# Attention with a token-mixer gate on one core: PSUM banks in one turn for scores and products, product blocks spread evenly, a tail in half-array products

## The chip, the cores and the metric

The kernel runs on one core of a Trainium2 chip. TensorE (PE) multiplies out of SBUF into eight PSUM banks of 128 x 512 fp32. VectorE (DVE), ScalarE (ACT) and GpSimd (POOL) read and write beside it, and SyncE (SP) issues most transfers. The metric is device time in microseconds (us), the median of the runs shown.

## The reference

`x` is 2048 tokens by 512 channels. With `xn = layernorm(x)` the kernel computes

```
s = softmax(q k^T / 4) v @ wo        # 32 heads of 16 channels, q, k, v = xn @ wqkv
g = silu((gelu(layernorm(xn)^T @ w1 + b1) @ w2 + b2)^T)   # a mixer over the tokens, F = 1792
out = x + s * g
```

All inputs are fp32. A product is made of three fp32r products of upper and lower parts (`three`, or the triple loops in `mixer` and `products`), so that every matrix product costs three passes.

## The kernel before, in words

**Opening (chunks of 512 tokens, `for c in range(NC)`).** Four blocks of 128 tokens are normalized (`Norm`: `stats`, `rsqrt`, `apply`, from L196 on), turned by TensorE (`turned`, L264), split into upper and lower parts, and multiplied with the weights of q and k (L303, eight groups of 12 passes) and of v (`v_product`, L336). q, k and v go to DRAM.

**Steady part (`for s in range(0, total + 1, 2)`).** The heads are taken in 16 pairs, `a` = 0 and 1, which use the upper and the lower half of the PE array's rows at the same time. One turn of the loop is a double step. For step `s` it makes the scores whose row maxima are sought (`max_of`: TensorE L394 into bank pool `ps_mx`, reduced by DVE L398), and, `LEAD` = 22 steps later, the scores again with the maximum folded in (`score`: TensorE L777 into `ps_sc`, exponentials by ACT L782). `values` (L793) multiplies the exponentials with v, four column tiles at once, into `ps_av`. A double step therefore has eight `m` (maxima), eight `s` (scores), two `V` (values), and `n` passes of the other work.

That other work is one long list (`everything`: `mixer`, then `rest`). It is drawn with `take` and consists of **blocks**: 14 of 48 passes (first matrix of the mixer, closed by `gelu`), 16 of 42 (second matrix, closed by `silu`), then 9 passes per output block (`products` with three of four head groups, closed by `part`), and at last the remaining 3 or 12 passes per output block (closed by `finish`). All passes of a block add up in one PSUM bank, `dn`. In the steady part each pass is split into two halves of 64 rows, `D` (`halves`, L944), one for each half of the array, so that every `D` runs beside an `m`, an `s` or another `D`. Outside the steady part it is one pass of 128 rows (`whole`, L903).

The order of a double step is written by hand in the strings of `ORDERS`: two rows of letters, one for each half of the array, read column by column, so one column is a pair of matmuls that run together; the two numbers are the columns before which a `V` stands. `count` says how many passes a double step takes: 6 as a rule, and 4 where a block ends or has just ended (`late`, with the tables `ENDS` and `BEGINS`), because the next block must wait until the single bank `dn` has been read out.

**PSUM.** Four pools: `ps_sc` 3 banks, `ps_mx` 3, `ps_av` 1, `ps_dn` 1.

**Tail (`else` branch, s >= NU = 512).** No maxima are left. Per half of a double step come score pairs, a `V` and up to 12 whole passes, three where an output block needs only its last head group. After the last `V` the last pair of heads is divided, multiplied with its share of `wo`, gated, added and stored (L1087 to the end).

Of the kernel before, what the change touches and what calls it, by code (L numbers as in the profile page):

```python
# [21 lines left out]
def tile_attention_token_mixer(ctx, tc, x, wqkv, wo, w1, b1, w2, b2, out):  # L22
# [131 lines left out]
    with (  # L154
        tc.tile_pool(name="pw", bufs=1) as pw,
        tc.tile_pool(name="px", bufs=5) as px,
        tc.tile_pool(name="pt", bufs=6) as pt,
# [23 lines left out]
        for part in range(3):  # L181
            for kd in range(ND):
                nm = ("raw", "wh", "wl")[(part * ND + kd) % 3]
# [4 lines left out]
        def w_upper(part):  # L188
            for kd in range(ND):
                nc.scalar.copy(wh[part][:, kd, :], raw_w[part, kd])  # L190

        def w_lower(part):
            for kd in range(ND):
                sub(nc.gpsimd, wl[part][:, kd, :], raw_w[part, kd], wh[part][:, kd, :])

        class Norm:  # L196


            def __init__(self, src, dst, then=None):
                self.src, self.dst, self.then = src, dst, then  # L200
# [7 lines left out]
            def rsqrt(self):  # L208
                ve = pst.tile([P, 4], F32, name="ve")
                r = self.r = pst.tile([P, 4], F32, name="r")  # L210
                t = pst.tile([P, 4], F32, name="t")
                nc.vector.tensor_scalar(ve, self.mv[:, :, 1], 1e-5, None, op0=OP.add)
                nc.scalar.sqrt(t, ve)
                nc.vector.reciprocal(r, t)
# [14 lines left out]
            def pieces(self):  # L229
                for b in range(4):  # L230
                    yield lambda b=b: self.stats(b)
                yield self.rsqrt
                for b in range(4):
                    yield lambda b=b: self.apply(b)

        def first(c):
# [4 lines left out]
            return Norm(lambda b: xr[4 * c + b], dst)  # L241
# [11 lines left out]
        def bank():  # L253

            i = turn_of[0] = (turn_of[0] + 1) % 8
            pl, nm = ((ps_sc, "sc"), (ps_mx, "mx"), (ps_dn, "dn"), (ps_av, "av"))[i % 2 if i < 6 else i - 4]
            return pl.tile([P, 512], F32, name=nm)

        for f in first(0).pieces():
            f()  # L260
        w_upper(0)
        xts_ = [[] for _ in range(NC)]

        def turned(c, db):  # L264
# [4 lines left out]
            t = pt.tile([P, 2, 512], F32R, name="xt")  # L269
            nc.scalar.copy(t[:, 0, :], ps)  # L270
            sub(nc.vector, t[:, 1, :], ps, t[:, 0, :])
            xts_[c].append(t)

        for c in range(NC):
            cs = slice(c * 512, (c + 1) * 512)
            for db in range(len(xts_[c]), ND):
                turned(c, db)
            if c == 0:

                nc.gpsimd.tensor_copy(pst.tile([P, 1], F32, name="hold"), xn[3][:, :1])  # L280
                w_upper(1)
                w_lower(0)
                w_lower(1)
# [5 lines left out]
            if c == 0:  # L289
                w_upper(2)  # L290
                w_lower(2)
# [35 lines left out]
            for f in todo[len(order) * per :]:  # L327
                f()
# [11 lines left out]
            pv = [bank()[:, :D] for _ in range(4)]  # L340
            if c + 1 < NC:
                for kd in range(ND):
                    for b in range(4):
                        v_product(b, kd)
                    if 0 < kd < ND - 1:
                        turned(c + 1, kd + 1)
            for b, ps in enumerate(pv):
# [5 lines left out]
                else:  # L353
                    v48 = pt.tile([P, 2, 512], F32R, name="xt").bitcast(F32).rearrange("p a b -> p (a b)")
                    v48 = v48[:, : NP * 48].rearrange("p (a b c) -> p a b c", b=3, c=DH)
                nc.gpsimd.memset(v48[:, :, 1, :], 1.0)
                nc.scalar.copy(v48[:, :, 0:3:2, :], ps.rearrange("p (a b c) -> p a b c", b=2, c=DH))
                nc.sync.dma_start(v_d[4 * c + b], v48.rearrange("p a b c -> p (a b c)"))
# [76 lines left out]
    def mixer():  # L435
        n = 0
        ub = []
        for i in range(NF + NB):
            nk = NB if i < NF else NF
            before = i < min(N_BEFORE, NF)  # L440
            if before and i % 2:
                ps = ps_av.tile([P, 512], F32, name="av")[:, :D]
            else:
                ps = ps_dn.tile([P, 512], F32, name="dn")[:, :D]
            for kb in range(nk):
# [5 lines left out]
                if i == NF and kb == NF - 1:  # L451
# [4 lines left out]
                    yield None  # L456
# [696 lines left out]
```

## Time and profile before

| | before |
|---|---|
| median of 3 runs | 1667.26 us (1667.24 to 1667.9) |
| the profiled execution | 1667.68 us |
| its span, first to last instruction | 1665.9 us |
| PE, DVE, ACT, POOL busy | 1644.1, 1426.0, 1194.2, 569.9 us |
| mean granted TensorE clock | 0.999 |

The profile is one execution on the chip. A row of the timeline has the start in us, the duration, the engine, the line of the kernel, the operation, what it writes `<-` what it reads, shapes and a count; what stands in brackets is the idle time before it and what ended it. PEld is the loading of weights, which runs beside PE. A busy PE may still be waiting: the end of a matmul is modelled, so the distance between starts tells more than the busy time.

### The profile page before, as it was taken

Reading aid. Unit: us, or ns where it says so; the run is one execution under the profiler, and the core shown is the slowest. Engines: PE = TensorE matmul, PEld = TensorE weight load, DVE = VectorE, ACT = ScalarE, POOL = GpSimd, SP = SyncE. Lnnn points to the kernel's source line nnn. Section 1 sums busy time; section 2 is a strip of 40 time slices with the busy share of each in tenths; the row PEclk is TensorE's granted clock in tenths of the full one; section 3 lists DMA queues with packets and bytes.
Section 4 is the critical chain, followed back from the end, with each engine's and each line's share of the span. In section 5 each row is a group of like instructions: output and inputs, shape, how many; then the busy total and the mean of one; then the engine's idle time right before and its main releaser. Section 6 shows DMA issues by size and latency. Waiting matters only on the chain.

```text
span 1665.9 us, 30703 instructions
## 1 busy us (share of the span) xinstructions
PE 1644.1 (99%) x11700; PEld 871.3 (52%) x11700; DVE 1426.0 (86%) x2482; ACT 1194.2 (72%) x2295; POOL 569.9 (34%) x671
## 2 busy tenths in 40 slices
PE   7999999999999999999999999999999999999997
PEld 6887645545545445554545454554545454444443
DVE  6555988888999899999999999999999999899945
ACT  3332277777777777777877777777777778888875
POOL 4223763433344332331322332222222322642420
PEclk9999999999999999999999999999999999999999
DMA  6468521415133141916151513224051515362346
GB/s 228 165 241 206 115 80 46 72 42 84 49 61 72 34 69 46 247 56 106 36 84 36 96 41 54 57 46 74 21 83 44 103 37 86 119 131 94 107 140 224
DMA packets 152175, 155.30 MB, mean 93 GB/s; under 512 B 51596, under 2 KB 109964, under 8 KB 148956
## 3 DMA queue, kind: packets, MB, share of 16 engines
q1 hardware_dynamic: 147612, 152.59, 38.1%
q8 instruction: 92, 1.51, 0.4%
q0 software_dynamic: 4416, 0.75, 0.3%
q14 instruction: 55, 0.45, 0.1%
HBM read 101.86 MB, written 50.32 MB: 91 GB/s over the span
## 4 chain that ended last, share of the span: by engine, by line
PE 96%; DVE 2%; DMA 1%; ACT 1%; issue 0%; POOL 0%; SPq 0%; DVEq 0%; POOLq 0%
PE av L793 30%; PE dn L944 23%; PE mx L394 17%; PE sc L777 13%; PE dn L903 3%; PE mx L303 2%; PE sc L303 2%; DVE mxp L398 1%; PE av L903 1%; PE dn L303 1%; PE av L303 1%; ACT prob L782 1%; PE mx L777 0%; PE sc L86 0%; PE sc L88 0%; PE sc L87 0%
## 5 line engine op out<-in xcount | busy, mean ns | idle before, releaser
L398 DVE TENSOR_REDUCE mxp<-mx 128x1 f32<-128x512 f32 x2004 | 1244.6, 684 | 134.9 <-PE mx L394 93.8
L782 ACT ACTIVATE prob<-sc 128x512 f32<-128x512 f32 x2004 | 1044.8, 605 | 296.2 <-PE sc L777 182.2
L777 PE MATMUL sc<-big 50*128 50x512 f32 x2004 | 755.6, 417 | 0.5
L394 PE MATMUL mx<-big 48*128 48x512 f32 x2004 | 738.6, 418 | 0.9
L793 PE MATMUL av<-prob,vp 128*32 128x512 f32 x4096 | 545.6, 605 | 0.0
L944 PE MATMUL dn<-hu,wh 64*128 64x512 f32 x1556 | 535.0, 404 | 0.0
L394 PEld LDWEIGHTS mx<-big 48*128 48x128 f32 x2004 | 358.6, 185 | 270.6 <-DVE mxp L398 248.7
L777 PEld LDWEIGHTS sc<-big 50*128 50x128 f32 x2004 | 358.6, 185 | 104.1 <-ACT prob L782 83.5
L944 PE MATMUL dn<-hu,wl 64*128 64x512 f32 x778 | 316.3, 407 | 0.0
L944 PEld LDWEIGHTS dn<-hu,wh 64*128 64x128 f32 x1556 | 284.4, 184 | 44.9 <-issue 23.8
L944 PEld LDWEIGHTS dn<-hu,wl 64*128 64x128 f32 x778 | 143.6, 185 | 108.1 <-issue 78.8
L793 PEld LDWEIGHTS av<-prob,vp 128*32 128x32 f32 x4096 | 80.9, 108 | 177.0 <-issue 166.1
L79 POOL TENSOR_TENSOR wl<-raw,wh 128x512 fp32r<-128x512 f32 x124 | 150.7, 1218 | 38.6 <-ACT wh L150 30.0
L148 POOL CAST wh<-raw 128x512 fp32r<-128x512 f32 (+1 forms) x107 | 62.1, 581 | 260.1 <-PE dn L944 177.7
L421 POOL CAST m<-f 16x128 fp32r<-16x128 f32 x32 | 9.0, 281 | 280.4 <-DVE f L410 280.4
L480 POOL TENSOR_TENSOR sq<-u 128x512 f32<-128x512 f32 x14 | 14.6, 1041 | 177.8 <-ACT u L479 177.8
L83 POOL DMA_DIRECT2D big<-m x128 | 67.7, 535 | 0.0
L944 PE MATMUL dn<-wh,hu 64*128 64x512 f32 x156 | 55.4, 408 | 0.0
L516 POOL TENSOR_SCALAR t<-t 128x512 f32<-128x512 f32 x16 | 23.8, 1490 | 79.9 <-ACT t L513 79.9
L79 POOL TENSOR_TENSOR hu<-hx,hu 128x512 fp32r<-128x512 f32 x16 | 20.3, 1291 | 53.5 <-ACT hu L246 53.5
L782 ACT ACTIVATE prob<-mx 128x512 f32<-128x512 f32 x44 | 28.1, 639 | 13.7 <-PE sc L777 13.6
L303 PE MATMUL mx<-xt,big 128*128 128x512 f32 x144 | 35.9, 399 | 0.0
(205 smaller groups left out, 1117.0 us busy)
## 6 DMA issues: line engine op xcount, KB each, us to landing
raw<-in_B_w_dram SPq DMA_DIRECT2D x104, 256.0 KB
big<-k_d SPq DMA_DIRECT2D x96, 128.0 KB
big<-q_d SPq DMA_DIRECT2D x96, 128.0 KB
q_d<-sg SPq DMA_DIRECT2D x16, 512.0 KB
k_d<-sg SPq DMA_DIRECT2D x16, 512.0 KB
num_d<-ev SPq DMA_DIRECT2D x30, 256.0 KB
u_d<-uo SPq DMA_DIRECT2D x14, 512.0 KB
hu<-u_d SPq DMA_DIRECT2D x14, 512.0 KB
```

The costliest lines, as they stand in the source:

```text
L79: eng.tensor_tensor(out=o, in0=a, in1=b.bitcast(F32), op=OP.subtract)
L83: queue.dma_start(dst.bitcast(F32), src.bitcast(F32))
L148: nc.gpsimd.tensor_copy(whs[n][:, :m, :], raws[n][:, :m, :])
L303: nc.tensor.matmul(ps, w[part][:, kd, m], xt[kd][:, z, :], start=w is wh and z == 0 and kd == 0, stop=w is wl and kd == ND - 1,)
L394: nc.tensor.matmul(ps, q[o : o + 48, r * P : (r + 1) * P], k[o : o + 48, c * 512 : (c + 1) * 512], start=True, stop=True,)
L398: nc.vector.tensor_reduce(mxp[u // 16][:, a, r % 8, c : c + 1], ps, axis=AX.X, op=OP.max)
L516: nc.gpsimd.tensor_scalar(t, t, 1.0, None, op0=OP.add)
L777: nc.tensor.matmul(ps, ks[p][o : o + 50, kb * P : (kb + 1) * P], qs[p][o : o + 50, at : at + 512], start=True, stop=True,)
L782: nc.scalar.activation(e, ps, AF.Exp, scale=scale)
L793: nc.tensor.matmul(av[32 * j : 32 * j + 32, :], vps[p][:, kb, 16 * a : 16 * a + 32], prob.pop((t, a, c)), start=kb == 0, stop=kb == NB - 1,)
L903: nc.tensor.matmul(ps, w(slice(0, P)), m(slice(0, P)), start=first, stop=last)
L944: made.append(lambda r=r, start=first and a == lead, stop=last and a != lead: nc.tensor.matmul(ps, w(r), m(r), start=start, stop=stop,))
```

## The change

Five parts.

1. `ps_dn` is gone. Its bank joins `ps_sc`, now four one-bank pools in a queue (`Banks`). `tile` takes the bank that was used longest ago and puts it at the end. `hold` takes a bank out for a whole product block; `back` returns it after the block's bank has been read out in the program's order.
2. `count` spreads a block's passes evenly (48 as 6, 6, 6, 5, 5, 5, 5, 5, 5 and 42 as 6, 6, 5, 5, 5, 5, 5, 5), except that blocks 4 to 6 still take 6 each time (4 to 7 before) and a block of 9 goes as 4 and 5. `ENDS`, `BEGINS`, `late` and `ended` are gone; `ORDERS` has new strings.
3. The tail takes its products through `a_half`. A block of 12 passes is still made whole, at every other half step. One of 3 passes is made in halves of 64 rows, as columns beside the scores; the halves of rows 64 to 127 come two half steps after those of rows 0 to 63, and the block's reader after them. All seven banks of scores and maxima are one queue there.
4. The opening normalizes blocks 0 and 1 first, loads and splits the weights of v first, multiplies blocks 0 and 1 with them (24 passes) before q and k, and puts 54 transposes of the identity, which nothing reads, on TensorE while it waits.
5. Small moves: the tanh of `silu` one place later, the reciprocals and divisions of the last head group earlier, one more output block (14, not 13) before the tail, the splits of the last weights later, zeroed rows instead of 96-row products.

```diff
-    ps_sc = pool("ps_sc", 3, space=PSUM)
-    ps_mx = pool("ps_mx", 3, space=PSUM)
-    ps_av = pool("ps_av", 1, space=PSUM)
-    ps_dn = pool("ps_dn", 1, space=PSUM)
+    class Banks:
+        def __init__(self, name, n):
+            self.free = [pool(f"{name}{i}", 1, space=PSUM) for i in range(n)]
+        def tile(self, shape, dtype, name):
+            self.free.append(self.free.pop(0))
+            return self.free[-1].tile(shape, dtype, name=name, tag="ps")
+        def hold(self, name):
+            p = self.free.pop(0)
+            return p.tile([P, 512], F32, name=name, tag="ps"), lambda: self.free.append(p)
+    ps_sc = Banks("ps_sc", 4)
+    ps_mx = Banks("ps_mx", 3)
+    ps_av = Banks("ps_av", 1)
...
+        busy(36)
+        one, two = first(0, range(2)), first(0, range(2, 4))
+        for f in one.pieces():
+            f()
...
+        ps0 = block_turn(0)
+        ps1 = block_turn(1)
+        busy(8)
+        two.stats(2)
+        two.stats(3)
+        w_upper(2, [0])
+        block_upper(0, ps0)
+        two.root()
...
+        w_lower(2, range(ND), nc.vector)
+        for kd in range(ND):
+            v_part(0, 0, wh, [kd])
+            busy((4, 4, 2, 0)[kd])
...
-                ps = ps_dn.tile([P, 512], F32, name="dn")[:, :D]
+                ps, back = ps_sc.hold("dn")
...
-        nc.scalar.activation(t, y, AF.Tanh)
+        later.append(lambda: nc.scalar.activation(t, y, AF.Tanh))
...
-    PARTS = NB // 2 + 5
+    PARTS = NB // 2 + 6
...
-    FULL = range(4, 8)
+    FULL = range(4, 7)
...
-        6: ("DDDDDDsmmsmsms", "msmssmmsDDDDDD", 4, 8),
+        5: ("DDDDDsmsmsmsm", "smsmsmsmDDDDD", 5, 8),
+        6: ("DDDDDDsmsmsmsm", "smsmmsmsDDDDDD", 4, 8),
...
-        return 4 if late or left in (7, 8) else 5 if left == 9 else max(0, min(6, left))
+        if left == 9:
+            return 4
+        return min(6, -(-left // -(-3 * left // 16))) if left > 0 and i not in FULL else max(0, min(6, left))
...
+    def a_half(one, two):
...
+        second, behind = second_rows.pop(0)
+        second_rows.append((last, then if first else []))
+        one, two = one + first, second + [lambda: None] * (len(first) - len(second)) + two
...
-            made = [heads[a][1] for a in range(2)]
-            n = len(made[0])
-            for i in range(n):
-                made[1][i]()
-                made[0][i]()
...
+            for i in range(2):
+                a_half(*(heads[a][1][2 * i : 2 * i + 2] for a in range(2)))
+                if not piece() and asides and s < total - 2:
+                    asides.pop(0)()
+                for v in range(t - 2, t + i):
+                    if (v, 0, 0) in prob:
+                        values(v)
```

What stands on TensorE where one 42-pass block follows another in the second matrix of the mixer. Before (L394 `m`, L777 `s`, L944 `D`; dn_16899 is the old block's bank and is not written any more here, dn_17547 the new block's):

```order
L793 MATMUL av_17416<-prob_17513,vp_15432 32x512
L394 MATMUL mx_17567<-big_1319,big_1318 128x512
L777 MATMUL sc_17570<-big_1428,big_1429 128x512
L944 MATMUL dn_17547<-hu_8753,wh_17231 128x512
L394 MATMUL mx_17575<-big_1319,big_1318 128x512
L944 MATMUL dn_17547<-hu_8753,wh_17231 128x512
L777 MATMUL sc_17579<-big_1428,big_1429 128x512
L944 MATMUL dn_17547<-hu_8753,wl_17232 128x512
L394 MATMUL mx_17584<-big_1319,big_1318 128x512
```

The same place after (L510 `m`, L894 `s`, L1047 `D`; dn_16912 is the old block's bank, dn_17560 the new one's):

```order
L510 MATMUL mx_17535<-big_1398,big_1397 128x512
L1047 MATMUL dn_16912<-hu_9504,wh_17000 128x512
L894 MATMUL sc_17539<-big_1507,big_1508 128x512
L1047 MATMUL dn_16912<-hu_9504,wl_17001 128x512
L510 MATMUL mx_17544<-big_1398,big_1397 128x512
L1047 MATMUL dn_16912<-hu_10155,wh_17000 128x512
L894 MATMUL sc_17548<-big_1507,big_1508 128x512
L1047 MATMUL dn_16912<-hu_10155,wh_17000 128x512
L510 MATMUL mx_17553<-big_1398,big_1397 128x512
L1047 MATMUL dn_16912<-hu_10155,wl_17001 128x512
L1047 MATMUL dn_17560<-hu_8915,wh_17235 128x512
L894 MATMUL sc_17568<-big_1507,big_1508 128x512
```

Before, a `V`, three columns without a `D`, a second `V` (its last matmul is the first row) and one more column stand between the old block's last `D` and the new block's first. After, the new block's first `D` stands in the column right behind the old block's last one, and the score beside it (sc_17568) is four columns behind sc_17539.

The tail on TensorE, at output blocks of three passes. Before (L777 scores in pools named sc and mx, L903 whole passes):

```order
L793 MATMUL av<-prob,vp 32x512 x4
L903 MATMUL dn<-wh,hu 128x512
L903 MATMUL dn<-wl,hu 128x512
L903 MATMUL dn<-wh,hu 128x512
L777 MATMUL mx<-big 128x512
L777 MATMUL sc<-big 128x512
L793 MATMUL av<-prob,vp 32x512 x4
```

After (L894 scores, L1095 halves of passes):

```order
L910 MATMUL av<-prob,vp 32x512 x4
L894 MATMUL sc<-big 128x512
L1095 MATMUL dn<-wh,hu 128x512
L894 MATMUL sc<-big 128x512
L1095 MATMUL dn<-wl,hu 128x512
L1095 MATMUL dn<-wh,hu 128x512 x2
L1095 MATMUL dn<-wl,hu 128x512
L894 MATMUL mx<-big 128x512
L1095 MATMUL dn<-wh,hu 128x512
L894 MATMUL mx<-big 128x512
```

Three whole passes and a score pair have become five columns of half-array matmuls, and each half step now has the same four scores.

More of the change, by code (lines that the diff above doesn't have):

```diff
@@ new lines, in v_out, with busy @@
+        def v_out(n, ps, v48, ones_in=False):
+            if not ones_in:
+                nc.gpsimd.memset(v48[:, :, 1, :], 1.0)
+            nc.scalar.copy(v48[:, :, 0:3:2, :], ps.rearrange("p (a b c) -> p a b c", b=2, c=DH))
+            nc.sync.dma_start(v_d[n], v48.rearrange("p a b c -> p (a b c)"))
+        v48s = [pst.tile([P, NP, 3, DH], F32, name="v48", bufs=2) for _ in range(2)]
+        for v48 in v48s:
+            nc.gpsimd.memset(v48[:, :, 1, :], 1.0)
+        idle = bank()
+        def busy(n):
+            for _ in range(n):
+                nc.tensor.transpose(idle[:, :P], ident, ident)
@@ L326, in tile_attention_token_mixer @@
                     w_split(2)
-            for f in todo[len(order) * per :]:
-                f()
+            left_ = todo[len(order) * per :]
+            if c > 0:
+                for f in left_:
+                    f()
             if c == NC - 1:
@@ L558, in two @@
             away.add((g, span))
-        after(8 if g < ND - 1 else 4, lambda: pieces.append(two))
+        after(8 if g < ND - 1 else 2, lambda: pieces.append(two))
     oc = {}
@@ L607, in parts @@
                 divided.add((g, span))
-        after(8 if now[0] < NU - 16 else 4, times)
+        after(8 if now[0] < NU - 16 else 2, times)
     def divisions():
@@ L960, in count, with each @@
                 break
-        if i in FULL:
-            return max(0, min(6, left))
-        return 4 if late or left in (7, 8) else 5 if left == 9 else max(0, min(6, left))
+        if left == 9:
+            return 4
+        return min(6, -(-left // -(-3 * left // 16))) if left > 0 and i not in FULL else max(0, min(6, left))
+    second_rows = [([], []), ([], [])]
+    long_ = []
+    def a_half(one, two):
+        got, then = [], []
+        def each(x, f):
+            if f:
+                then.append(f)
+            else:
+                got.append(x)
+        if not long_:
+            take(3 * ND, each)
+            if len(got) == 3 * ND:
+                long_.append(True)
+        else:
+            long_.clear()
+        first, last = [], []
+        if len(got) == 3:
+            for ps, w, m, start, stop in got:
+                for a, made in ((0, first), (1, last)):
+                    r = slice(64 * a, 64 * a + 64)
+                    made.append(lambda ps=ps, w=w, m=m, r=r, start=start and a == 0, stop=stop and a == 1: nc.tensor.matmul(
+                        ps, w(r), m(r), start=start, stop=stop,
+                    ))
+        second, behind = second_rows.pop(0)
+        second_rows.append((last, then if first else []))
+        one, two = one + first, second + [lambda: None] * (len(first) - len(second)) + two
+        for i in range(max(len(one), len(two))):
+            for of in (one, two):
+                if i < len(of):
+                    of[i]()
+            if i == len(second) - 1:
+                for f in behind:
+                    f()
+        if not first:
+            for x in got:
+                whole(x, None)
+            for f in then:
+                f()
     def items(s, a):
@@ L1000, in tile_attention_token_mixer @@
             steady[0] = True
-            late = ended[0]
-            one, two, then = halves(lead, count(late))
+            one, two, then = halves(lead, count())
             made = [dict(D=part, m=heads[a][0], s=heads[a][1]) for part, a in ((one, lead), (two, 1 - lead))]
-            first, second, *places = order(len(one), t, late, bool(then))
+            first, second, *places = order(len(one))
             if one:
@@ L1018, in tile_attention_token_mixer @@
                         of[kind].pop(0)()
-                if "D" in kinds and not two:
-                    for f in then:
-                        f()
-                    then = []
             for f in then:
```

225 lines of the change are left out of this document (130 added, 95 removed).

## The prediction

> **What bounds the kernel now.** The page comes first: who is busy, and what stands on the chain that ended last.
>
> ```profile
> span 1665.9 us, 30703 instructions
> PE 1644.1 (99%) x11700; PEld 871.3 (52%) x11700; DVE 1426.0 (86%) x2482; ACT 1194.2 (72%) x2295; POOL 569.9 (34%) x671
> PE 96%; DVE 2%; DMA 1%; ACT 1%; issue 0%; POOL 0%; SPq 0%; DVEq 0%; POOLq 0%
> ```
>
> TensorE is the path, and DVE is near behind. A busy PE hides short waits, so I read starts in the timeline instead. The rows are the first matmuls of a `V`: two neighbours of a step with six passes, two of a step with four, then the edges of a 42-pass block, a 48-pass block, a 9-pass block, and the first and the last `V` of the steady part.
>
> ```profile
> 1000.46 1.06 PE L793 MATMUL av<-prob,vp 128*32 128x512 f32 x8
> 1002.59 1.06 PE L793 MATMUL av<-prob,vp 128*32 128x512 f32 x8
> 1006.14 1.07 PE L793 MATMUL av<-prob,vp 128*32 128x512 f32 x8
> ...
> 1028.85 1.07 PE L793 MATMUL av<-prob,vp 128*32 128x512 f32 x8
> 1030.76 1.07 PE L793 MATMUL av<-prob,vp 128*32 128x512 f32 x8
> 1034.12 1.06 PE L793 MATMUL av<-prob,vp 128*32 128x512 f32 x8
> ...
> 1041.61 1.06 PE L793 MATMUL av<-prob,vp 128*32 128x512 f32 x8
> ...
> 1086.30 1.07 PE L793 MATMUL av<-prob,vp 128*32 128x512 f32 x8
> ...
> 565.87 1.07 PE L793 MATMUL av<-prob,vp 128*32 128x512 f32 x8
> ...
> 616.73 1.06 PE L793 MATMUL av<-prob,vp 128*32 128x512 f32 x8
> ...
> 1509.72 1.06 PE L793 MATMUL av<-prob,vp 128*32 128x512 f32 x8
> ...
> 1520.66 1.07 PE L793 MATMUL av<-prob,vp 128*32 128x512 f32 x8
> ...
> 216.40 1.06 PE L793 MATMUL av<-prob,vp 128*32 128x512 f32 x8
> ...
> 1587.00 1.07 PE L793 MATMUL av<-prob,vp 128*32 128x512 f32 x8
> ```
>
> With six passes (the strings of `ORDERS`) there are 4 columns from the first `V` to the second and 10 to the next: 2.13 and 3.55 us. So a column costs (3.55 - 2.13) / 6 = 0.236, and a `V` 2.13 - 4 x 0.236 = 1.185. Three columns give 1.89, and the row pair at 1028.85 has 1.91. I call this the **column price**: what TensorE needs when nothing makes it wait. A double step costs 2 x 1.185 + (8 + n) x 0.236, which is 5.67 for six passes, 5.44 for five, 5.20 for four.
>
> Now the measured blocks. The 42-pass block (8 double steps, 106 columns) took 44.69 against 43.98, 0.71 over; the 48-pass block (9 double steps, 120 columns) 50.86 against 49.65, 1.21 over; the 9-pass block (2 double steps, 25 columns) 10.94 against 10.64, 0.30 over. The steps with six are at the price, so the excess lies where blocks meet and four passes stand in a step. Over the whole steady part, 244 double steps with 1276 passes, the price is 488 x 1.185 + 3228 x 0.236 = 1340.1; measured are 1370.6. **30.5 us** is all that a better order can win there.
>
> Why four passes cost more than their columns, and what five will meet, DVE shows:
>
> ```profile
> 1002.25 4.95 DVE L398 TENSOR_REDUCE mxp<-mx 128x1 f32<-128x512 f32 x8 [0.71 <-PE mx L394]
> 1007.12 0.21 DVE L413 TENSOR_REDUCE neg<-mxp 128x16 f32<-128x64 f32 x1
> 1007.43 0.20 DVE L410 STREAM_TRANSPOSE f<-neg 32x32 f32<-32x32 f32 x1
> ...
> 1012.91 0.63 DVE L410 STREAM_TRANSPOSE f<-neg 32x32 f32<-32x32 f32 x3
> ```
>
> Eight reductions take 4.95 and every eighth double step adds 0.41, the next one 0.63: 5.08 a step on average. That leaves 0.12 at four passes, 0.36 at five, 0.59 at six. A step of four has no room for the additions; a step of five has.
>
> **The change part by part.**
>
> *Spreading (steady part).* The number of double steps is fixed by the scores. Five more passes are drawn before 1587, and five 128-row passes at its end, less one column of scores: 9 columns, 2.1 us added. The removed waits are the 30.5, and the order of the changed program has only step forms with six, five or (9-pass blocks) four passes. Against this stands the new wait. A new block holds the oldest score bank, so its first step's scores find their banks one place earlier in the queue: at the place shown, four columns (4 x 0.236 = 0.94 us) behind the score that used the bank. Before, such a meeting stands at 1036.34:
>
> ```profile
> 1035.12 0.73 PE L777 MATMUL sc<-big 50*128 50x512 f32 x2
> 1035.69 2.06 ACT L782 ACTIVATE prob<-sc 128x512 f32<-128x512 f32 x4 [0.81 <-PE sc L777]
> 1036.34 0.18 PEld L777 LDWEIGHTS sc<-big 50*128 50x128 f32 x1 [0.45 <-ACT prob L782]
> 1037.61 0.71 ACT L512 ACTIVATE ev<-dn,b2h 128x512 f32<-128x512 f32 x1
> ```
>
> The score's bank is used again 1.22 us after its start (1035.12 to 1036.34), 0.57 of it until the exponential starts. A score in the middle of a run is followed by its exponential some 0.46 after its start, an estimate from the row lengths (a matmul of 0.40 and a hand-over of 0.05 as from the exponential's end to 1036.34): 1.11. The wait is thus between 0.17 and 0.28 per change of block. I take 0.2: at that place the score follows another without a `V` between, so it is nearer to the lower end. About 41 blocks change in the steady part: 8.2 us. What is queued behind is TensorE's whole stream, so all of it counts. The block's own reader (0.71) stands on ACT behind the step's exponentials; its bank is wanted only after the next `V`.
>
> What else stays: maxima that come in steps of five or four, between 0 and 0.3 in some 30 places, taken as 0.15, 4.5; and half of the 8.2 us of excess that lies outside the 34 blocks priced above (16 x 0.71 + 6 x 1.21 + 12 x 0.30 = 22.3), since the first four blocks keep their sixes: 4. Left are 16.7 of 30.5. **Steady part: -13.8 + 2.1 = -11.7.** Between its ends: -24 (no new wait at all) and 0 (0.5 per change).
>
> *Tail.* The half steps with three passes:
>
> ```profile
> 1623.82 1.06 PE L793 MATMUL av<-prob,vp 128*32 128x512 f32 x8
> ...
> 1626.14 1.06 PE L793 MATMUL av<-prob,vp 128*32 128x512 f32 x8
> ...
> 1628.91 1.07 PE L793 MATMUL av<-prob,vp 128*32 128x512 f32 x8
> ...
> 1646.07 3.35 PE L793 MATMUL av<-prob,vp 128*32 128x512 f32 x24
> ```
>
> 5.09 a double step, where two `V` and ten columns are 4.73: 0.36 goes into the change between whole-array passes and half-array scores. From 1587.00 to the last `V`'s end (1649.42) 62.4 passed; 24 `V`, 41 score pairs, 75 passes and 12 small transposes (about 1.3) are 57.1 (counted in the program's order), so 5.3 is excess. After: 24 `V`, 117 columns (17 half steps of 5, two of 14, two of 2) and the transposes, 57.3. The columns are no fewer, as unpaired ends fill what nine passes less give. The gain is the excess: 0.36 in some eight double steps goes, the rest (ACT behind at the start and at the last scores) stays. **-2.8**, between -5 and +2. ACT stays covered: four exponentials at 2.06 / 4 = 0.52 need 2.1 of a half step's 2.37.
>
> *Opening.*
>
> ```profile
> 4.24 0.66 DVE L205 BATCH_NORM_STATS2 st<-xr 128x6 f32<-128x512 f32 x1
> 4.94 0.18 DVE L206 BATCH_NORM_AGGREGATE mv<-st 128x2 f32<-128x6 f32 x1
> ...
> 7.66 0.17 DVE L212 TENSOR_SCALAR ve<-mv 128x4 f32<-128x4 f32 x1
> ...
> 9.12 1.91 DVE L222 TENSOR_SCALAR xn<-xr,mv,r 128x512 f32<-128x512 f32 x4
> ...
> 12.22 0.69 DVE L79 TENSOR_TENSOR xt<-mx,xt 128x512 fp32r<-128x512 f32 x1 [1.19 <-ACT xt L270]
> ...
> 13.77 4.20 PE L303 MATMUL mx<-xt,big 128*128 128x512 f32 x12
> ...
> 17.81 2.89 PE L303 MATMUL dn<-xt,big 128*128 128x512 f32 x12
> ...
> 20.54 2.88 PE L303 MATMUL av<-xt,big 128*128 128x512 f32 x12
> ```
>
> The second block's statistics end at 5.12, so normalizing starts at 5.12 + 9.12 - 7.66 = 6.6. DVE then sets the pace: two normalizations 0.95 (half of 1.91), two statistics 1.7, the lower parts of two turned blocks 1.7 (four pieces of half the size of the row at 12.22, an estimate of 0.42 each), the second root and its small steps 1.3, two normalizations 0.95, four lower parts of v's weights 4 x 0.69 = 2.8: done at about 16.0. The last eight of the 24 v passes wait for these and take 8 x 0.227 (2.73 / 12, from 17.81 to 20.54): 17.8, when q begins. Before, at 17.81, 12 passes were behind. **12 x 0.227 = -2.7**, between -4.2 (DVE late nowhere) and 0. Transposes added on PE lie in its waits; b1, b2 and v's stores pass SP later, and nobody waits for them there.
>
> *The small moves* lie beside TensorE's stream at 72% of ACT and 34% of POOL; I price them at nothing. If that cover failed, a late tanh would hold POOL's chain and the weights' splits, inside the excess above.
>
> **Sum.** -11.7 - 2.8 - 2.7 = -17.2: 1667.68 - 17.2 = 1650.5 for an execution like the profiled one, which was 0.4 above the median. **Forecast 1650.0.**
>
> **Rivals.**
>
> *No new wait.* The exponential is early enough at each change, and DVE's additions fit: only some 4 us of the excess stay. 30.5 - 4 - 2.1 + 5.5 = 29.9 less: 1637.4. For it, that the steps of six, which are as full, have no excess; against it, the row at 1036.34.
>
> *DVE sets the step, and the spreading does not spread.* The reductions and their additions, 5.08 of a step of five's 5.44, lose their place when maxima come closely and the mean double step stays at 5.62. Then spreading changes nothing and only the 9 columns count: 1667.3 + 2.1 - 5.5 = 1663.9. For it, the 0.30 over in the 9-pass blocks at 4.5 passes a step; against it, that the order of five has at most one `m` a column and 0.36 spare.
>
> *The clock stays low.* The first twelve passes at 13.77 took 4.20 against 2.89 later: TensorE was slow there although it had been turning blocks since 9.80. If dummy transposes do not raise its rate, the v passes lose about as much, 1.3: 1651.3. The Trainium skill (TensorE: Matmul & The Clock Gate, Part 4: PE-mode transpose) says that the full clock does not engage for transposes; the rows at 13.77 and 17.81 agree with that, but also with a rise that comes late.
>
> *The held bank costs more (slower).* If the finished block's reader (0.71 on ACT) comes ahead of the exponential whose bank the next score needs, or ACT is behind by as much, each change costs 0.2 + 0.71. Then 1650.0 + 41 x 0.71 = 1679. It decides from 0.2 + 17.2 / 41 = 0.62 per change on. Against it, the reader stands behind that step's exponentials, and ACT is busy 72%.
>
> **How the numbers follow.** A measurement of this kernel can tell 0.2%, 3.3 us, from no change: faster means below 1663.9, slower above 1670.6. Chances: forecast 0.45 (1643 to 1657), no new wait 0.17, low clock 0.15, DVE 0.13, held bank 0.10. Faster is the first three and half of DVE, 0.84; the same is the other half and a little of the held bank, 0.07; slower 0.09. The range takes in no new wait and DVE, 1637 to 1664, and leaves out the held bank and the outer edges.
>
> **What would show it.** Right: two neighbouring `V` of a step of five 5.44 apart in sum; a 42-pass block in 44.3; scores behind a new block's first `D` about 0.2 late, with PEld waiting for ACT's exponential; a half step of the tail near 2.37; q's first group at 17.8. Wrong: steps of five at 5.6, waits for reductions inside them, changes of block above 0.6, or a tail whose `V` lie over 2.6 apart.

## The result, and the profile after

| | before | after |
|---|---|---|
| median of 4 runs | 1667.58 us (1667.24 to 1667.91) | 1650.76 us (1650.28 to 1651.38) |
| the profiled execution | 1667.68 us | 1650.5 us |
| its span | 1665.9 us | 1648.7 us |
| mean granted TensorE clock | 0.999 | 0.996 |

The ratio is 0.9899, with a 95% interval from 0.9882 to 0.9917: 16.8 us faster, where 17.2 was forecast for the profiled execution. The total is right, but it is right because errors cancel. The span is therefore cut at the same four marks as in the prediction: the first `V`, the `V` that ends the steady part, the end of the last `V`, and the end of the span.

| | before | after | change | forecast |
|---|---|---|---|---|
| start to the first `V` | 216.4 | 212.9 | -3.5 | -2.7 |
| steady part | 1370.6 | 1356.1 | -14.5 | -11.7 |
| tail, to the last `V`'s end | 62.4 | 57.7 | -4.7 | -2.8 |
| last `V`'s end to the span's end | 16.5 | 22.0 | +5.5 | no term |
| sum | 1665.9 | 1648.7 | -17.2 | -17.2 |

First the page of the changed kernel: span, busy shares, and the chain that ended last.

```profile
span 1648.7 us, 31003 instructions
PE 1633.3 (99%) x11800; PEld 883.2 (54%) x11800; DVE 1423.6 (86%) x2500; ACT 1187.2 (72%) x2301; POOL 564.1 (34%) x667
PE 96%; DMA 1%; DVE 1%; POOL 1%; issue 0%; ACT 0%; SPq 0%; DVEq 0%; POOLq 0%
```

TensorE is still the path, and the page alone shows no new bound. The starts of the `V` in the timeline show more: two neighbours of a step of five and the next one, then two changes of block, eight double steps apart, then the marks of the steady part.

```profile
1005.69 0.64 PE L910 MATMUL av<-prob,vp 128*32 128x512 f32 x4
1009.23 0.64 PE L910 MATMUL av<-prob,vp 128*32 128x512 f32 x4
1011.12 0.64 PE L910 MATMUL av<-prob,vp 128*32 128x512 f32 x4
...
1016.53 1.06 PE L910 MATMUL av<-prob,vp 128*32 128x512 f32 x8
...
1060.79 0.64 PE L910 MATMUL av<-prob,vp 128*32 128x512 f32 x4
...
212.91 0.64 PE L910 MATMUL av<-prob,vp 128*32 128x512 f32 x4
...
1568.97 0.64 PE L910 MATMUL av<-prob,vp 128*32 128x512 f32 x4
```

A step of five takes 3.54 + 1.89 = 5.43 (forecast 5.44), and a 42-pass block 1060.79 - 1016.53 = 44.26 (forecast 44.3, before 44.69). Call a `V` with the columns up to the next `V` a **group**. Counted over the trace, the 37 groups of nine columns that hold a change of block are 3.56 long in the mean, where their columns cost 1.185 + 9 x 0.236 = 3.31: 0.25 per change, 9.2 in all. The forecast was 0.2 and 8.2.

The timeline at the change shows that wait: two scores of the old step, their exponentials, and the loading of the weights of the first score beside the new block.

```profile
1017.87 0.40 PE L894 MATMUL sc<-big 50*128 50x512 f32 x1
...
1018.30 1.08 ACT L899 ACTIVATE prob<-sc 128x512 f32<-128x512 f32 x2 [0.55 <-PE sc L894]
1018.35 0.39 PE L894 MATMUL sc<-big 50*128 50x512 f32 x1
...
1018.95 0.18 PEld L894 LDWEIGHTS sc<-big 50*128 50x128 f32 x1 [0.20 <-ACT prob L899]
```

The bank is used again 1.08 after its score (forecast 1.11), and the score is 0.15 behind the `D` beside it (at 1018.80). The list of waits of PEld says the same of the whole run; before, these two rows held 83.5 us (145 times) and 248.7 us (345 times).

```profile
PEld sc L894 <- ACT prob L899: 232.4, 343, 0.8
...
PEld mx L510 <- DVE mxp L514: 145.0, 182, 0.8
```

Weight loads wait more often for exponentials and less for reductions. Most of this costs nothing: the two rows hold 377 us, and the whole steady part lies only 13.8 us over the column price.

Two `V` of the tail, with the halves of a three-pass block between them, are 2.36 apart (forecast 2.37):

```profile
1617.10 1.06 PE L910 MATMUL av<-prob,vp 128*32 128x512 f32 x8
1619.46 1.07 PE L910 MATMUL av<-prob,vp 128*32 128x512 f32 x8
```

The end is what the forecast lacked. First SP's queue: the loads of y for three output blocks in turn, the last block's gate, its store, and at last the eight gate loads (L882).

```profile
1615.23 0.32 SPq L864 DMA_DIRECT2D u<-y_d  x1
...
1619.75 0.32 SPq L864 DMA_DIRECT2D xt<-y_d  x1
...
1624.60 0.32 SPq L864 DMA_DIRECT2D u<-y_d  x1
1624.98 0.41 SPq L866 DMA_DIRECT2D sq<-g_d  x1
...
1630.49 0.33 SPq L873 DMA_DIRECT2D out_dram<-u  x1
1630.92 3.72 SPq L882 DMA_DIRECT2D prob<-g_d  x8
```

Between these loads SP stood at the load of y until the store of the same buffer had landed, up to 3.2 us each time. The output blocks took 4.5 to 4.9 us each in this way, where TensorE's half step is 2.36. This pace is not new. Before the change, two loads of y in a row:

```profile
1638.20 0.32 SPq L747 DMA_DIRECT2D xt<-y_d  x1
...
1642.67 0.32 SPq L747 DMA_DIRECT2D u<-y_d  x1
```

What is new is where the row of blocks stands against the last `V`: its first store was issued 22.1 us ahead of the last `V`'s end before (at 1627.27), and 18.0 us ahead of it after (at 1608.74).

Then VectorE: the last output block's `finish` (L870, L871), the reciprocals of the last heads (L750), and a gate product of the end (L1245).

```profile
1629.04 0.69 DVE L870 TENSOR_TENSOR sq<-dn,sq 128x512 f32<-128x512 f32 x1 [3.41 <-DMA sq<-g_d]
...
1630.38 0.27 DVE L750 RECIPROCAL rq<-sc 128x8 f32<-128x8 f32 x2
...
1638.01 0.69 DVE L1245 TENSOR_TENSOR prob<-mx,prob 128x512 f32<-128x512 f32 x1 [2.96 <-PE av L102]
```

And TensorE: the last two `V`, the transposes that the reciprocals read, the next work after them, and two of the closing products.

```profile
1624.78 1.92 PE L910 MATMUL av<-prob,vp 128*32 128x512 f32 x16
1627.49 0.66 PE L747 MATMUL sc<-ident,ev 128*128 128x128 f32 x4 [0.78 <-ACT ev L643]
1630.97 0.80 PE L761 MATMUL sc<-ident,t 128*128 128x128 f32 x2 [2.82 <-DVE t L752]
...
1633.27 0.63 PE L102 MATMUL sc<-uo,big 128*128 128x512 f32 x1
1633.69 0.63 PE L103 MATMUL sc<-uo,big 128*128 128x512 f32 x1
```

The last output block's gate was loaded late (issued at 1624.98), so its `finish` came 2.3 us after the last `V`'s end. Before, it came 3.1 us ahead of that end (1646.33 against 1649.42):

```profile
1646.33 0.69 DVE L753 TENSOR_TENSOR sq<-dn,sq 128x512 f32<-128x512 f32 x1 [2.79 <-DMA sq<-g_d]
```

Two things stand behind it: the reciprocals on VectorE, and on SP, behind its store, the gate loads. TensorE paused 2.8 us, and its products then came 0.42 apart instead of 0.23, because the granted clock was 0.5 from 1629.6 to 1636.4. The 5.5 us can be divided: from the last `V`'s end to TensorE's first matmul on the reciprocals (L761) 4.3 us instead of 2.0, from there to the end of the last product 9.2 instead of 7.1, which is the low clock, and 8.5 instead of 7.4 behind it.

### The profile page after: what moved, and what is told of

Same layout as the page of the kernel before. It is cut to its first block, busy times and chain, and to the rows that moved or that the text cites. A ratio compares the mean times of both kernels' runs of the same rounds, so it can differ in the third digit from the quotient of the medians.

```text
span 1648.7 us, 31003 instructions
## 1 busy us (share of the span) xinstructions
PE 1633.3 (99%) x11800; PEld 883.2 (54%) x11800; DVE 1423.6 (86%) x2500; ACT 1187.2 (72%) x2301; POOL 564.1 (34%) x667
## 4 chain that ended last, share of the span: by engine, by line
PE 96%; DMA 1%; DVE 1%; POOL 1%; issue 0%; ACT 0%; SPq 0%; DVEq 0%; POOLq 0%
PE av L910 30%; PE dn L1047 23%; PE sc L894 17%; PE mx L510 14%; PE sc L412 3%; PE mx L412 2%; PE dn L1018 2%; PE av L1018 1%; PE av L412 1%; DMA sq<-g_d 0%; DMA out_dram<-u 0%; PE sc L103 0%; PE sc L101 0%; PE sc L102 0%; PE mx L103 0%; PE mx L101 0%
## 5 line engine op out<-in xcount | busy, mean ns | idle before, releaser
L510 PE MATMUL mx<-big 48*128 48x512 f32 x2004 | 761.3, 416 | 0.0
L894 PE MATMUL sc<-big 50*128 50x512 f32 x2004 | 739.7, 412 | 0.2 <-ACT prob L899 0.2
L1047 PE MATMUL dn<-hu,wh 64*128 64x512 f32 x1556 | 530.7, 408 | 0.0
L894 PEld LDWEIGHTS sc<-big 50*128 50x128 f32 x2004 | 358.2, 186 | 260.1 <-ACT prob L899 232.4
L510 PEld LDWEIGHTS mx<-big 48*128 48x128 f32 x2004 | 358.0, 186 | 161.7 <-DVE mxp L514 145.0
L1047 PEld LDWEIGHTS dn<-hu,wh 64*128 64x128 f32 x1556 | 277.4, 184 | 89.1 <-issue 64.9
L1047 PE MATMUL dn<-hu,wl 64*128 64x512 f32 x778 | 308.4, 396 | 0.0
L1047 PEld LDWEIGHTS dn<-hu,wl 64*128 64x128 f32 x778 | 143.7, 185 | 13.6
L595 POOL TENSOR_TENSOR sq<-u 128x512 f32<-128x512 f32 x14 | 14.5, 1039 | 182.3 <-ACT u L594 182.3
L1047 PE MATMUL dn<-wh,hu 64*128 64x512 f32 x162 | 52.9, 392 | 0.0
L412 PE MATMUL sc<-xt,big 128*128 128x512 f32 x192 | 46.1, 389 | 0.0
L412 PEld LDWEIGHTS sc<-xt,big 128*128 128x128 f32 x192 | 36.0, 188 | 7.5
```

The lines of the kernel that those rows point to most:

```text
L412: nc.tensor.matmul(ps, w[part][:, kd, m], xt[kd][:, z, :], start=w is wh and z == 0 and kd == 0, stop=w is wl and kd == ND - 1,)
L510: nc.tensor.matmul(ps, q[o : o + 48, r * P : (r + 1) * P], k[o : o + 48, c * 512 : (c + 1) * 512], start=True, stop=True,)
L894: nc.tensor.matmul(ps, ks[p][o : o + 50, kb * P : (kb + 1) * P], qs[p][o : o + 50, at : at + 512], start=True, stop=True,)
L1047: made.append(lambda r=r, start=first and a == lead, stop=last and a != lead: nc.tensor.matmul(ps, w(r), m(r), start=start, stop=stop,))
```

## The experiments

The theory for the end: output blocks go through a ring of four pairs of buffers (load, finish, store, load again). The two half steps by which the reader of a three-pass block is late, and the ring's own pace, push the last finish past the last `V`. The rival: the end is long for another reason (the clock, the queue of the gate loads alone). For the steady part the theory was the forecast's: the wait per change (0.2 forecast, 0.25 measured) is the score that waits for its exponential.

Every run's four parts, from its own trace (us):

| run | to the first `V` | steady | tail | end | profiled | median (range, 4 runs) |
|---|---|---|---|---|---|---|
| after | 212.9 | 1356.1 | 57.7 | 22.0 | 1650.5 | 1650.8 (1650.3 to 1651.4) |
| no_dummies | 213.5 | 1356.0 | 59.6 | 20.7 | 1651.5 | 1653.6 (1651.5 to 1654.0) |
| fours | 212.2 | 1367.2 | 57.9 | 22.0 | 1661.1 | 1661.2 (1660.3 to 1662.3) |
| own_bank | 213.1 | 1400.1 | 57.6 | 21.9 | 1694.5 | 1694.5 (1694.3 to 1694.7) |
| maxima_first | 213.0 | 1354.9 | 57.6 | 22.6 | 1649.9 | 1649.5 (1648.0 to 1649.9) |
| values_early | 212.9 | 1364.8 | 57.9 | 21.6 | 1658.8 | 1659.0 (1657.9 to 1659.2) |
| end_queue | 213.0 | 1356.4 | 60.3 | 19.7 | 1651.1 | 1652.1 (1651.1 to 1653.5) |
| end_finish | 212.4 | 1356.5 | 57.6 | 19.5 | 1647.8 | 1647.7 (1647.5 to 1648.7) |
| end_both | 212.3 | 1356.8 | 58.5 | 19.0 | 1648.3 | 1649.1 (1648.3 to 1650.1) |
| ring_early | 213.1 | 1355.6 | 59.5 | 18.8 | 1648.8 | 1649.8 (1648.8 to 1650.8) |
| tail_whole | 212.1 | 1355.7 | 59.8 | 16.2 | 1645.5 | 1646.6 (1645.5 to 1651.1) |
| ring_lag | 212.8 | 1356.7 | 57.6 | 17.7 | 1646.6 | 1646.1 (1645.5 to 1646.6) |
| best | 213.2 | 1355.0 | 57.6 | 16.3 | 1643.8 | 1643.4 (1642.7 to 1643.9) |

Kernels with the same opening reach the first `V` between 212.1 and 213.2, so half a microsecond in that column says nothing.

**no_dummies: do the idle transposes raise TensorE's rate?**

```diff
-            for _ in range(n):
+            for _ in range(0):
                 nc.tensor.transpose(idle[:, :P], ident, ident)
```

> The 54 transposes of the identity in the opening are left out; everything that the output needs is kept. If they raise TensorE's rate, the first twelve v passes go back to about 0.35 each (4.20 for twelve, as at 13.77 before), q's first group starts 1 to 2 us later than 17.66, and the time is 1652 to 1653. Rival, in which the rate comes from something else (the v passes simply come later than the passes at 13.77 did): q's first group stays at 17.7 and the time at 1650.8.

TensorE's rows in the opening, first of the changed kernel, then without the transposes: four block transposes, four v passes, and q's first group.

```profile
7.26 0.66 PE L304 MATMUL sc<-ident,xn 128*128 128x128 f32 x4
...
12.54 1.18 PE L344 MATMUL mx<-wvh,xt 128*128 128x512 f32 x4
...
17.66 2.88 PE L412 MATMUL sc<-xt,big 128*128 128x512 f32 x12
```

```profile
7.25 1.09 PE L304 MATMUL sc<-ident,xn 128*128 128x128 f32 x4 [7.25 <-DVE xn L246]
...
13.05 1.62 PE L344 MATMUL mx<-wvh,xt 128*128 128x512 f32 x4
14.51 0.60 PE L304 MATMUL av<-ident,xn 128*128 128x128 f32 x4
...
18.61 2.88 PE L412 MATMUL sc<-xt,big 128*128 128x512 f32 x12
```

They do. With them four transposes take 0.66 from the first on; without them 1.09, and the rate comes only at about 14.5. q begins 0.95 later. (The profile's granted clock reads 1.00 in both openings, so the rate is read from the rows.) The rival "the clock stays low" priced a low rate nearly right (1.3), but its condition is not met: transposes that nothing reads do raise the rate. What the 0.95 is worth in the end is not shown: the first `V` comes 0.6 later, hardly more than the scatter of that column. The Trainium skill (TensorE: Matmul & The Clock Gate, Part 4: PE-mode transpose) says that the full clock does not engage for transposes; these rows differ from that, 0.66 against 1.09 for the same four. What the median of 1653.6 has beyond the 1 us of the profiled execution isn't settled.

**fours: the spreading alone undone.**

```diff
-        return min(6, -(-left // -(-3 * left // 16))) if left > 0 and i not in FULL else max(0, min(6, left))
+        if left > 0 and i not in FULL and (0 < i and left == n or left in (7, 8)):
+            return 4
+        return max(0, min(6, left))
```

> The spreading alone is undone: blocks of 48 and 42 passes begin and end with steps of four and take six in between, as before, on the new turn of banks and with the new strings. If the steps of four have no room for the reductions and their additions, a 42-pass block costs 0.4 to 0.7 more than 44.2 and a 48-pass block about 1 more: 10 to 18 us in all, 1661 to 1669. Rival, in which the excess of before came from the lone product bank and the gaps kept for it: blocks stay at 44.2, and the time within 2 us of 1650.8.

It took 10.4 more than the changed kernel, all of it in the steady part, at the lower end of what was expected. But a step of four as such costs little. A block now has three groups of ten maxima and scores with eight `D`; two of them mostly cost 0.05 to 0.12 over their columns and the one at the change 0.55. The timeline there shows three exponentials in a row and the new block's score behind the last but one:

```profile
1024.04 1.58 ACT L899 ACTIVATE prob<-sc 128x512 f32<-128x512 f32 x3 [0.37 <-PE mx L510]
...
1025.17 0.18 PEld L894 LDWEIGHTS sc<-big 50*128 50x128 f32 x1 [0.24 <-ACT prob L899]
```

So spreading is worth about 10 of the 14.5, some 7 of it at the changes. That it helps there by thinning out the scores is what this row suggests; the two runs on the 0.25 below qualify it.

**own_bank: product blocks with their own bank again.**

```diff
-    ps_sc = Banks("ps_sc", 4)
+    ps_sc = Banks("ps_sc", 3)
+    ps_dn = Banks("ps_dn", 1)
...
-                ps, back = ps_sc.hold("dn")
+                ps, back = ps_dn.hold("dn")
...
-            ps_sc.free += ps_mx.free
-            ps_mx.free = ps_sc.free
+            ps_sc.free += ps_mx.free + ps_dn.free
+            ps_mx.free = ps_dn.free = ps_sc.free
```

> The product blocks get a bank of their own again (scores three, maxima three, values one, products one) until the tail, with the spread steps kept. If the turn of banks is what lets blocks follow without a gap, the new block's first pass waits for the old block's reader, which stands behind the step's last exponentials on ACT: 0.7 to 1.3 per change instead of 0.25, so 18 to 43 us more over 41 changes, 1669 to 1694, with TensorE waiting for the reader of dn. Rival, in which the reader is early enough: the 0.25 goes as well, and the time is about 1641.

44 more, 1.1 per change beyond the 0.25, and TensorE's list of waits in the steady part names the readers of the block: its three largest rows, all readers on ACT, hold 40.7 us. Two of them:

```profile
PE dn L1048 <- ACT ev L628: 17.1, 15, 1.1
PE dn L1048 <- ACT t L831: 12.3, 13, 0.9
```

So without the turn of banks a change without a gap costs more than the gaps of before did. A lone bank with spread steps and with a gap kept for the reader was not run.

**maxima_first and values_early: what is the 0.25?** In the steps that begin a block, first the maxima come ahead of the scores; then, in addition, the first `V` stands before the second column.

```diff
+    BEGIN = {
+        4: ("DDDDssmmsmms", "msmsmmssDDDD", 4, 7),
+        5: ("DDDDDsmsmsmsm", "msmsmsmsDDDDD", 5, 8),
+        6: ("DDDDDDsmsmsmsm", "msmsmsmsDDDDDD", 4, 8),
+    }
```

In values_early the numbers at the ends of these rows are 1, 7; 1, 8; and 1, 8.

> In the steps that begin a block, the half of the array that makes no product begins with a maximum and not with a score, so that each score there comes one column later (0.236). If the 0.25 per change is a score waiting for the exponential that empties its bank, nearly all of it goes: the groups of nine columns at a change fall from 3.56 to 3.33-3.40, and the time by 6 to 9 us, to 1642-1645. Rival, in which the wait is for the reductions or for the array itself: the groups stay at 3.56 or grow, since two maxima then stand in neighbouring columns, and the time is 1650 to 1656.

The groups at a change fell only from 3.56 to 3.53, and the steady part by 1.1: the rival's case, although the time, 1649.5, lies just under the rival's range. The wait for the exponential is gone, and one column later, at the same place in the block, a maximum waits for its reduction for nearly as long:

```profile
1018.95 0.18 PEld L510 LDWEIGHTS mx<-big 48*128 48x128 f32 x1 [0.20 <-DVE mxp L514]
```

> As the run that began with a maximum, and in addition the first V of a step that begins a block stands before its second column, not before its fifth. If the 0.25 per change is TensorE running into two things that are both late by about as much (the exponential that empties the score bank, and, right behind it, the reductions), a V there gives both 1.07 us: the whole 0.25 goes at some 37 changes, 8 to 9 us, 1641 to 1643. Rival, in which the reductions run without a break through the columns around the change and only move their wait: 1648 to 1651.

It became 8 us slower, which neither expected. Counted over its trace, the groups around a change are now six and seven columns long: 37 of six columns with two scores cost 0.10 over their columns, 26 of seven with five scores 0.29, and in the 9-pass blocks 14 of six with five scores 0.53. So the theory of one late score falls. An explanation that fits, but that no run here shows, is that scores and maxima come so closely around a change that ACT (0.5 per exponential) and VectorE (0.6 per reduction) are both late there, and that a column or a `V` moved only chooses which of them TensorE meets. How the 0.25 divides between the two stays open.

**end_queue, end_finish, end_both: which chain holds the end?** The gate loads from POOL's queue; the last finish behind the reciprocals; both.

```diff
-            nc.sync.dma_start(gates[b], g_d[b])
+            nc.gpsimd.dma_start(gates[b], g_d[b])
...
-            yield lambda n=n, ps=ps: finish(n, ps), back
+            if n < NB - 1:
+                yield lambda n=n, ps=ps: finish(n, ps), back
+            else:
+                yield lambda n=n, ps=ps, back=back: last.append(lambda: (finish(n, ps, nc.gpsimd), back())), lambda: None
...
-    for f in left:
+    for f in left + last:
         f()
```

> The eight gate loads of the end are issued by POOL and no longer by SP, where they stand behind the last four stores; nothing else is moved. If SP's queue holds them up, the second gate product no longer waits until 1638.0; products and VectorE set the end then: 1.3 us less (1649.5). If SP's queue were the whole of the 5.5 us: 4 to 6 less. Rival, in which the loads are not late for anybody: no change, 1650.8.

A miss. The end is 2.3 shorter, but the tail 2.5 longer. Three views of this run: POOL's first gate loads, VectorE's last finish, and the load on the DMA engines from 1620 to 1632.

```profile
1619.07 1.18 POOL L882 DMA_DIRECT2D prob<-g_d  x2 [34.03 <-PE dn L1095]
```

```profile
1632.11 0.69 DVE L870 TENSOR_TENSOR sq<-dn,sq 128x512 f32<-128x512 f32 x1 [4.90 <-DMA sq<-g_d]
```

```profile
DMA packets 1750, 4.15 MB, mean 346 GB/s; under 512 B 247, under 2 KB 247, under 8 KB 1748
```

Off SP's queue, the gate loads start at 1619, 12 us sooner, and fill the DMA engines (346 GB/s in the mean, and 355 to 437 in most slices from 1624 on) just when the ring needs them; its last load, issued at 1626.5, was waited for until 1632.1, and the last scores waited 1.6 us for a bank. The Trainium skill (DMA: Bandwidth & Descriptors, Issuing engines are not separate DMA queues) says that transfers of all issuing engines run on the same 16 DMA engines. The trace agrees: from 1620 to 1632 the packets of POOL's queue took 51.0% of the time of the 16 engines and those of SP's queue 45.9%. SP's order had protected the ring.

> The last output block's two operations are put behind the reciprocals and their copies on VectorE, its addition on POOL; the gate loads stay behind its store on SP. If the finish holds up VectorE, the reciprocals begin near 1628.2 instead of 1630.4, TensorE's pause shrinks from 2.8 to about 1, but the gates still come at 1638 or later: 0 to 0.5 slower or the same, 1650.8 to 1651.3. Rival, in which VectorE's queue alone makes the 5.5 us: 2 to 4 less, 1647 to 1649.

3.1 less, more than expected. With the finish moved, its store moves too, so that the gate loads no longer stand behind it. VectorE and SP:

```profile
1627.96 0.28 DVE L750 RECIPROCAL rq<-sc 128x8 f32<-128x8 f32 x2 [2.56 <-PE sc L747]
```

```profile
1626.77 5.24 SPq L884 DMA_DIRECT2D prob<-g_d  x8
```

Both start sooner (1630.4 and 1630.9 in the changed kernel), so this run cannot tell the two chains apart, although its time lies in the rival's range.

> Both edits together. If the end waits for whichever of the two chains is later (reciprocals behind the finish, gates behind the store), only both together show the gain: 2.5 to 4.5 less, 1646.3 to 1648.3, with last V to end near 18.5. Rival, in which only one of them counts: the same as that one alone.

1649.1: not as good as the finish alone, since the gate loads from POOL again cost the tail 0.9 and give the end only 0.5. The end, 19.0, is near the expected 18.5, but the finish alone had nearly all of that, so the expectation falls. Both chains start sooner as soon as the last finish is moved; how much each of them counts, these three runs do not show.

**ring_early and tail_whole: is it where the ring begins, and how late its readers are?**

```diff
-            after(4, lambda: own_done.append(True))
+            after(2, lambda: own_done.append(True))
```

> The second half of the output blocks may begin two half steps after the last head group's own rows were sent, not four. If the ring of output buffers (store, load, finish, store) sets when the last finish is, it ends 2.4 us sooner against the last V, and the end shrinks from 22.0 to 18-19.5: 1647.3 to 1648.3. Rival, in which the last blocks' transfers or the low clock set the end and not where the ring begins: 22.0 stays, and TensorE may wait for the rows: 1650.8 to 1652.

Two half steps were also what the kernel before had here; that the change made them four is not in its list of parts. The end shrinks as expected (18.8), but the tail grows by 1.8: the ring, begun sooner, is still slower than TensorE, and a held bank now stops the scores (1.5 us of wait at one place). Only 1 us is won, and the two kernels' executions overlap.

```diff
-        if len(got) == 3:
+        if False:
```

> Tail blocks of three passes are made as whole passes again, with their reader right behind them and no longer two half steps later; everything else is as changed. If the halves save the change between whole-array and half-array work, each such half step goes from 2.36 to about 2.55 (2 us more in ten of them); if the late reader is what pushes the ring into the end, the end shrinks by 3 to 5 us: in sum 1 to 3 us less, 1648 to 1650. Rival, in which the ring is set by its loads and not by the two half steps: 2 us more, 1652.8.

Half of the tail's gain goes (two `V` of a half step 2.57 apart, below, instead of 2.36), and the end is back at 16.2, under the 16.5 of before: the rival is out. The rows are two `V`, then the last finish.

```profile
1612.39 1.07 PE L910 MATMUL av<-prob,vp 128*32 128x512 f32 x8
1614.96 1.06 PE L910 MATMUL av<-prob,vp 128*32 128x512 f32 x8
```

```profile
1624.07 0.69 DVE L870 TENSOR_TENSOR sq<-dn,sq 128x512 f32<-128x512 f32 x1 [1.98 <-DMA sq<-g_d]
```

So the halves with a reader two half steps later save 2.1 in the tail and cost 5.8 at the end: as it stands, this part of the change loses 3.7 us. One of the four executions took 1651.1 at a mean granted clock of 0.996, which is also the changed kernel's; the other three had 0.999 and lie between 1645.5 and 1647.1.

**ring_lag: is the ring's pace set by SP standing in front of its own store?**

```diff
-        load_out(n + 4)
+        if n > 0:
+            load_out(n + 3)
```

> Each finish of an output block starts the loads for the block three places on, not four, so that on SP's queue a load of y no longer stands right behind the store that must empty its buffer, but behind the next block's store. Halves, two half steps of delay and everything else are as changed. If SP standing in front of its own store is what makes the ring slower than a half step (4.4 us per block of loads against 2.36), the last finish no longer waits for its gate, the end shrinks from 22.0 to 16.5-18, and the tail keeps its 57.7: 1645 to 1646.5. Rival, in which the two half steps of delay alone push the last finish into the end, however fast the ring: the end stays at 21 or more, 1650 to 1651.

Yes. SP's loads of y in this run, and the last finish:

```profile
1614.47 0.38 SPq L864 DMA_DIRECT2D u<-y_d  x1
...
1616.80 0.35 SPq L864 DMA_DIRECT2D xt<-y_d  x1
...
1619.49 0.32 SPq L864 DMA_DIRECT2D u<-y_d  x1
```

```profile
1624.88 0.69 DVE L870 TENSOR_TENSOR sq<-dn,sq 128x512 f32<-128x512 f32 x1 [0.67 <-DMA sq<-g_d]
```

Loads come 2.3 to 2.7 us apart, a half step of the tail, where the changed kernel had 4.5 to 4.9. The end is 17.7 and the tail keeps its 57.6, two half steps of delay and all. So the delay hurts only because the ring is slow: with loads at TensorE's pace, the ring may start as late as in the changed kernel.

**best: both kernels beaten.** The ring one place later, maxima first, and six gate loads ahead of the last store:

```diff
+                    if s == total - 2:
+                        load_gates(NB // 2, NB - 2)
                     now[0] = s + 1
                     run_later()
-            if s == total - 2:
-                load_gates(NB // 2, NB - 2)
```

> Three edits together: the loads of the output ring one place later, a maximum first in the steps that begin a block, and six of the eight gate loads of the end one place earlier on SP, ahead of the last store. If the gates behind that store are what is left in the end (17.7 against 16.5 before the change), the second gate product no longer waits 1.4 us and the end falls to 16.3; with 1.1 less in the steady part the time is 1643 to 1644. Rival, in which the gate loads ahead only take the DMA engines from the ring's last load and TensorE waits for it: the tail grows by 1 to 2.5, 1645 to 1647.

```profile
1622.51 2.77 SPq L883 DMA_DIRECT2D prob<-g_d  x6
```

1643.4, with a ratio to before of 0.9855 (0.9839 to 0.9871); the changed kernel had 0.9899 (0.9882 to 0.9917). The end is 16.3 as expected, and the tail pays nothing: the ring's last load was issued 4 us ahead of these six (at 1618.53).

## Why the prediction was right, and where only in sum

- **Spreading** (-11.7, measured -14.5). The mechanism held in the main: steps of five at the column price, and at a change a score that waits for its exponential, 0.25 in sum. What was mis-sized is "what else stays": of the 13.8 us that lie over the price, 9.2 are at changes, and the remaining 4.6 stood as 8.5 in the sum. "Maxima that come in steps of five" were taken at 0.15 in 30 places and are hardly to be seen. The runs add that this score is not the whole reason: with it out of the way, a maximum waits there for its reduction, and only 0.03 of a group's 0.25 goes.
- **Tail** (-2.8, measured -4.7). Half steps of 2.36 came as forecast (2.37). "The rest (ACT behind at the start and at the last scores) stays" was wrong: 57.7 was measured where the columns cost 57.3, so hardly anything of the excess stayed.
- **The failing step.** The prediction priced the halves by TensorE's columns and gave no price to the sentence that the block's reader comes two half steps later, nor to what that reader starts: a store, and on SP the next block's loads behind it. The finish, its store, the loads and the gate loads of the end all move with it. It cost 5.5 at the end, 2.1 of it because the granted clock fell to 0.5 when TensorE had paused, which the prediction did not price there either. The ring was as slow before, but its first store stood 22.1 us ahead of the last `V`'s end and now stands 18.0 ahead. Two edits of the change hold it back: the later reader (without it, in tail_whole, 23.9 ahead) and the mark moved from two half steps to four (moved back, in ring_early, 22.1 ahead). tail_whole and ring_lag each remove most of the 5.5, by different edits of the same chain, and with the pause at 0.64 the clock stays at 1.00 up to the last product.
- **Opening** (-2.7, measured -3.5, of which half a microsecond is scatter). q began at 17.66, forecast 17.8.
- **The small moves** at nothing: no stage shows one, and no run took one of them out alone.
- **Rivals.** No new wait (1637.4) is out by the 0.25; DVE sets the step is out by 5.43 per step of five; the held bank at 0.2 + 0.71 is out as it stands, but own_bank shows that a price of that kind, 1.35, is what a single product bank would have paid. The low clock is out by no_dummies' rows, not by the time, which is only 0.5 from the rival's 1651.3.

The three gains together were 22.7, 5.5 more than forecast, and the missing term was 5.5. That the sum met the time to 0.1 us is chance.

## What to carry to other kernels

When a reader of results is moved later, follow what it starts and not only what it waits for: here a store, a load behind it in the same queue, and a buffer that comes round four blocks later. A load that stands right behind the store of its own buffer makes the issuing queue wait for that store; one place later cost nothing here and doubled the ring's pace. A queue that looks like a hindrance can also be what keeps a bulk of transfers off the DMA engines until the small ones are through.

## What the runs showed of the hardware

- Transposes of the identity raise TensorE's rate: four block transposes took 0.66 us behind them and 1.09 without.
- After a pause of 2.82 us (1628.15 to 1630.97) the closing products came 0.42 apart for 5 us, then 0.23 again; after pauses of 0.64, in tail_whole and ring_lag, they came 0.23 apart from the second on. The length of one pause is not all that counts: in no_dummies the granted clock was 0.5 behind a pause of 1.84, and in end_both, where TensorE paused 2.32 a little later (behind its first matmuls on the reciprocals), it was 1.00 behind the pause.
- With the gate loads of 2.1 MB in flight, the wait for a 256 KB load of the ring grew: issued 1626.5 and used 1632.1, 5.6 us, against 4.1 (1624.98 to 1629.04) in the changed kernel.
